# Gate and value as seven block products over parts of 512 tokens, with four of twelve column blocks beside the attention

## The chip, the core and the metric

The kernel runs on one core of a Trainium2 chip, in one launch. The metric is the device time of that launch in microseconds (us). The core has five instruction streams that run side by side and wait for each other through semaphores: PE (TensorE, matrix products into PSUM), DVE (VectorE), ACT (ScalarE), POOL (GpSimd) and SP (SyncE, which here only issues DMA transfers). PE, DVE and ACT can read or write PSUM as the program uses it here; POOL works on SBUF alone.

## The reference

Attention with feature maps in place of a softmax, then a gated layer on its output (cut to what is computed):

```python
def phi(x):
    proj = np.einsum('bhsd,df->bhsf', x, w_phi)
    proj = proj - np.max(np.abs(proj), axis=-1, keepdims=True)
    return np.concatenate([np.exp(proj), np.exp(-proj)], axis=-1)
q_p, k_p = phi(q), phi(k)                    # batch 8, heads 8, 576 tokens, 64 -> 2 x 128
kv = np.einsum('bhsf,bhsd->bhfd', k_p, v)
num = np.einsum('bhsf,bhfd->bhsd', q_p, kv)
den = np.einsum('bhsf,bhf->bhs', q_p, np.sum(k_p, axis=2))[..., None] + 1e-06
x = (num / den)                              # as (4608 tokens, 512)
xn = x / np.sqrt(np.mean(x * x, -1, keepdims=True) + 1e-06) * rms_g
g, val = xn @ w_gate, xn @ w_val             # 512 x 1536 each
out = (g / (1 + np.exp(-g)) * val) @ w_out   # 1536 x 512
```

The three large weights arrive as float64: the kernel reads them as pairs of 32-bit words and decodes them to float32 itself. The other inputs are float32.

## The kernel before, in words

Every matrix product in reduced float32 is made of three matmuls: each operand is split into a high part (a cast on ACT) and a low part (a subtraction on DVE or POOL; `_split`, L59), and high x high, high x low and low x high are summed in PSUM. There are three stages.

**Attention** (first 500 us). 32 pairs of heads pass a pipeline: `front` (transposes and projections), `mid` (exponentials, the sum over tokens), `back` (numerator and denominator), `last` (division, store of x to `xs` in DRAM). Between them run the pieces that decode weights, one per pair (`decode_pieces`), and *fill* units: for a block of 288 tokens whose x is in DRAM, `fill` (L460) splits x, and a unit (L467) computes one of the first `J1` = 3 column blocks of 128 columns, for gate or value, without the norm, in 12 matmuls 288 wide (L474), copies the sum out of PSUM (L477) and stores it to `gvs`. 16 blocks x 3 x 2 = 96 units. The rest of them run after the last pair (L533).

**Gate/value** (about 610 to 1067 us). 12 parts of `T` = 384 tokens. `prep` (L145) squares x, sums the squares by a matmul with ones, takes root and reciprocal (L159, L160), scales x (L162) and splits it. `gv` (L576) goes through the other nine column blocks: 12 matmuls 384 wide for the gate into one PSUM bank, 12 for the value into another (L588); then `hidden` (L569): SiLU on ACT, a product on DVE (L573), a store to `hs`. `gv_raw` (L593) fetches a block that the fill units computed, multiplies it by the reciprocal norm on DVE (L596) and finishes it in the same way; three per part. Pieces that decode w_out run beside this, and `load_o` prepares weights of the output stage.

**Output** (about 1067 us to the end). 18 groups of 256 tokens, each a 2 x 2 block product made of seven products instead of eight (`omm`, L737: 18 matmuls 256 wide each), with sums and differences of blocks formed on DVE and splits by ACT, DVE and POOL (L672 to L684).

The order of instructions on each engine is not that of the source: the framework simulates the program when it is built and places what it finds ready first. `late` ties some pieces behind the last instruction of an engine. A tile pool with `bufs=n` keeps n buffers of a name; a new one waits until the oldest is read. Each engine works off its own order strictly.

Of the kernel before, what the change touches and what calls it, by code (L numbers as in the profile page):

```python
# [82 lines left out]
def kernel(ctx: ExitStack, tc: tile.TileContext, q, k, v, w_phi,  # L83
# [13 lines left out]
    J1 = 3  # L97
    T = 384
    NB = N // T
    TF = S // 2  # L100
# [19 lines left out]
    x_ctx = ExitStack()  # L120
    wfp = x_ctx.enter_context(tc.tile_pool(name="wfp", bufs=1))
    wf1 = [[wfp.tile([128, NC, J1 * 128], F32R, name=f"f{n}{i}") for i in range(2)] for n in "gv"]
    xm = x_ctx.enter_context(tc.tile_pool(name="xm", bufs=1))
    xops = [x_ctx.enter_context(tc.tile_pool(name="xo0", bufs=1))]
    xips = [x_ctx.enter_context(tc.tile_pool(name="xip", bufs=1))]
# [13 lines left out]

    def fetch(bk, n=T):  # L140
        x = xips[-1 if bk % 2 else 0].tile([128, NC * T], F32, name="x")[:, 0:NC * n].rearrange("p (c t) -> p c t", c=NC)
        nc.sync.dma_start(out=x, in_=xsv[:, :, bk * n:(bk + 1) * n])
        return x

    def prep(bk, x, pool, name):  # L145
        ss = xm.tile([128, T], F32, name="ss", bufs=1)
        nc.scalar.activation(ss, x[:, 0], AF.Square)
        for c in range(1, NC):
            sq = xm.tile([128, T], F32, name="sq", bufs=1)
            nc.scalar.activation(sq, x[:, c], AF.Square)  # L150
            nc.gpsimd.tensor_tensor(ss, ss, sq, ALU.add)  # L151
        sp = pool.tile([128, T], F32, name=name)
        sh = xm.tile([128, T], F32R, name="sq", bufs=1)
        sl = xm.tile([128, T], F32R, name="fo", bufs=3)
        _split(nc, sh, sl, ss, lo_eng=nc.gpsimd)
        nc.tensor.matmul(sp[:, 0:T], ones, sh, start=True, stop=False)
        nc.tensor.matmul(sp[:, 0:T], ones, sl, start=False, stop=True)
        ri = xm.tile([128, T], F32, name="ri", bufs=2)
        nc.scalar.activation(ri, sp[:, 0:T], AF.Sqrt, scale=1.0 / DM, bias=eps)  # L159
        nc.vector.reciprocal(ri, ri)  # L160
        for c in range(NC):
            nc.vector.scalar_tensor_tensor(x[:, c], x[:, c], g[:, c:c + 1], ri, ALU.mult, ALU.mult)  # L162
        xhl = xops[bk % len(xops)].tile([128, 2, NC, T], F32R, name="xb")
        _split(nc, xhl[:, 0], xhl[:, 1], x, lo_eng=nc.gpsimd)
        return xhl[:, 0], xhl[:, 1], ri
# [334 lines left out]
    for i in range(PR + 3):  # L500
# [26 lines left out]
        if i == PR - 5:  # L527
            x0 = fetch(0)
# [272 lines left out]
```

## Time and profile before

| what | value |
|---|---|
| median of 3 runs | 1345.85 us (1344.51 to 1346.44) |
| span of the profiled execution | 1345.4 us |
| granted TensorE clock, mean | 0.991 |
| HBM read, written | 126.04 MB, 69.50 MB |
| longest waits of PE, in total | 9.8 us, 9 times (fill units, for a split of x on DVE); 7.6 us, once (output stage, for a cast on ACT); 4.6 us, once (gate/value, for a weight's cast on ACT) |

The page of the profile gives for the profiled execution its span, from the first to the last instruction, and no other time. A row of a group has the source line, the engine, the operation, output and inputs by the program's names, shapes, the count, then busy time in us, the mean duration of one in ns, and the engine's idle time just before them with what ended it. A row of a timeline has the start and the duration in us. A row of stretches has for each engine the busy time in us and the number of instructions, then the granted clock, the DMA share and GB/s. A row of the chain of waits has a start, a duration, an engine, a tile and a line.

### The profile page before, as it was taken

What the parts mean: (1) busy time and instruction counts of PE and PEld (TensorE: products, weight loads), DVE (VectorE), ACT (ScalarE), POOL (GpSimd) and SP (SyncE); (2) the same over time, 40 slices, a digit from 0 to 9 for tenths busy, and PEclk for the clock granted to TensorE, in tenths of its full rate; (3) what the DMA queues carried; (4) which work ended last, traced back from release to release, by engine and by line L of the source; (5) the groups of instructions that cost most, each with busy time, mean ns of one, the idle gap of its engine ahead of it and who ended that gap; (6) DMA issues with size and microseconds to landing.
All of it is one profiled execution on the core that took longest, in us unless ns stands there. A gap on an engine that the chain in (4) does not pass through costs nothing.

```text
span 1345.4 us, 25468 instructions
## 1 busy us (share of the span) xinstructions
PE 1291.3 (96%) x9396; PEld 1275.3 (95%) x9396; DVE 914.7 (68%) x1301; ACT 710.0 (53%) x1510; POOL 619.6 (46%) x568
## 2 busy tenths in 40 slices
PE   7989999999999997998999999999999799999998
PEld 7889899999999887998999999999999799999998
DVE  7899888778778762114566656655343489999995
ACT  5988877778778772334434434443332234344332
POOL 3766565555556660000223222222221078878885
PEclk9999999999999898999999999999999999999999
DMA  5455656565556434437454454454333434454351
GB/s 162 125 144 158 162 159 166 168 170 167 161 151 162 125 113 144 150 128 203 145 171 145 157 176 154 133 169 151 110 123 100 158 116 136 132 172 137 126 176 60
DMA packets 204523, 197.21 MB, mean 147 GB/s; under 512 B 69553, under 2 KB 186417, under 8 KB 204401
## 3 DMA queue, kind: packets, MB, share of 16 engines
q1 hardware_dynamic: 194896, 190.88, 47.0%
q10 hardware_dynamic: 9504, 4.72, 1.2%
q8 instruction: 74, 1.21, 0.4%
q14 instruction: 49, 0.39, 0.1%
HBM read 126.04 MB, written 69.50 MB: 145 GB/s over the span
## 4 chain that ended last, share of the span: by engine, by line
PE 80%; DVE 7%; DMA 5%; ACT 4%; issue 2%; POOL 2%; SPq 0%; ACTq 0%; DVEq 0%; POOLq 0%
PE fp L588 15%; PE gp L588 15%; PE fp L474 10%; PE acc L351 6%; PE gd L737 5%; PE gz L737 5%; PE gy L737 5%; PE sm L415 3%; PE fp L737 2%; PE pp L311 2%; PE fp L415 2%; PE pp L313 2%; PE pp L312 2%; PE sm L298 2%; PE sm L364 2%
## 5 line engine op out<-in xcount | busy, mean ns | idle before, releaser
L380 POOL TENSOR_TENSOR ql<-eq,qh 128x256 fp32r<-128x256 f32 x256 | 217.1, 879 | 67.2 <-issue 38.2
L61 POOL TENSOR_TENSOR xo<-st,xo 128x768 fp32r<-128x768 f32 x54 | 125.0, 2328 | 94.0 <-ACT xo L60 92.2
L588 PE MATMUL fp<-xb,wg 128*128 128x384 f32 x864 | 163.0, 336 | 4.6 <-ACT wg L60 4.6
L588 PE MATMUL gp<-xb,wv 128*128 128x384 f32 x864 | 161.5, 334 | 0.0
L588 PEld LDWEIGHTS fp<-xb,wg 128*128 128x128 f32 x864 | 151.9, 189 | 5.1 <-ACT wg L60 4.9
L573 DVE TENSOR_TENSOR h<-sl,gp 128x384 f32<-128x384 f32 x108 | 59.5, 551 | 135.0 <-PE gp L588 71.2
L588 PEld LDWEIGHTS gp<-xb,wv 128*128 128x128 f32 x864 | 150.8, 188 | 0.0
L571 ACT ACTIVATE sl<-fp 128x384 f32<-128x384 f32 x108 | 52.7, 489 | 167.4 <-PE fp L588 148.6
L54 POOL TENSOR_TENSOR wa<-raw,wa 128x192 f32<-128x192 f32 (+1 forms) x112 | 67.4, 622 | 159.5 <-issue 56.7
L351 PE MATMUL acc<-vm,ek 128*128 128x65 f32 x1024 | 131.6, 271 | 0.0
L315 DVE TENSOR_REDUCE mx<-pp 128x4 f32<-128x512 f32 (+1 forms) x160 | 100.5, 631 | 42.4 <-PE pp L313 41.1
L351 PEld LDWEIGHTS acc<-vm,ek 128*128 128x128 f32 x1024 | 127.8, 194 | 0.3 <-ACT ek L338 0.2
L60 ACT CAST xo<-st 128x768 fp32r<-128x768 f32 x54 | 43.4, 835 | 153.1 <-DVE st L675 76.9
L61 POOL TENSOR_TENSOR xb<-x,xb 128x1536 fp32r<-128x1536 f32 x12 | 42.7, 3562 | 152.0 <-ACT xb L60 152.0
L151 POOL TENSOR_TENSOR ss<-ss,sq 128x384 f32<-128x384 f32 x36 | 37.5, 1041 | 154.4 <-ACT sq L150 154.4
L474 PE MATMUL fp<-xo,fg 128*128 128x288 f32 x576 | 95.9, 303 | 9.8 <-DVE xo L61 9.8
L376 ACT ACTIVATE qh<-sm 128x512 fp32r<-128x512 f32 (+1 forms) x192 | 97.1, 506 | 0.0
L474 PEld LDWEIGHTS fp<-xo,fg 128*128 128x128 f32 x576 | 81.8, 190 | 13.2 <-DVE xo L61 12.2
L474 PE MATMUL fp<-xo,fv 128*128 128x288 f32 x576 | 92.5, 299 | 0.0
L61 POOL TENSOR_TENSOR xo<-ht,xo 128x768 fp32r<-128x768 f32 x36 | 91.6, 2545 | 0.0
L311 PE MATMUL pp<-wh,th 128*128 128x256 f32 x288 | 88.6, 309 | 2.7 <-DVE yr L318 2.1
L375 ACT ACTIVATE eq<-sm 128x512 f32<-128x512 f32 x128 | 78.2, 611 | 13.1 <-PE sm L364 12.0
(163 smaller groups left out, 3589.1 us busy)
## 6 DMA issues: line engine op xcount, KB each, us to landing
hs<-h SPq DMA_DIRECT2D x144, 192.0 KB
ht<-hs SPq DMA_DIRECT2D x18, 1536.0 KB
gvs<-fo SPq DMA_DIRECT2D x96, 144.0 KB
gvr<-gvs SPq DMA_DIRECT2D x36, 384.0 KB
rc<-di SPq DMA_DIRECT2D x32, 288.0 KB
x<-xs SPq DMA_DIRECT2D x16, 576.0 KB
x<-xs SPq DMA_DIRECT2D x12, 768.0 KB
kt<-in_k_dram SPq DMA_DIRECT2D x32, 256.0 KB
```

Of the source, the lines that this page charges most:

```text
L54: nc.gpsimd.tensor_tensor(a[:, h], lf[:, h], a[:, h], ALU.mult)
L61: (lo_eng or nc.vector).tensor_tensor(lo, x, hi.bitcast(F32), ALU.subtract)
L311: nc.tensor.matmul(o, th[:, cs], wh, start=True, stop=False)
L315: nc.vector.tensor_reduce(mx[:, 0:2 * m], pp[:, 0:2 * m], axis=AX.X, op=ALU.max, apply_absolute_value=True)
L351: nc.tensor.matmul(acc[:, sg, h], e[h][:, sg, j], vm[:, h, j], start=False, stop=(h == 1 and j == T0 - 1))
L375: nc.scalar.activation(ei[:, sg], yi, AF.Exp, scale=1.0 - 2.0 * sg)
L376: nc.scalar.activation(hi[:, sg], yi, AF.Exp, scale=1.0 - 2.0 * sg)
L380: nc.gpsimd.tensor_tensor(lo[:, sg, cs], ei[:, sg, cs], hi[:, sg, cs].bitcast(F32), ALU.subtract)
L415: nc.tensor.matmul(o[:, 0:SH], a[:, h, sg], e[:, sg, h, cs], start=(i == 0), stop=(i == 5))
L474: nc.tensor.matmul(fp[:, 0:TF], w, xx[x][:, c], start=(i == 0), stop=(i == 3 * NC - 1))
L588: nc.tensor.matmul(gp[:, 0:T], w, e[:, c], start=(i == 0), stop=(i == 3 * NC - 1))
L737: nc.tensor.matmul(place[n], a[:, kp], w[:, o], start=(first and kp == 0 and i == 0), stop=(kp == KP - 1 and i == 2), skip_group_check=True)
```

## The change

The gate and value products take the form that the output stage has already. A part is now 512 tokens, and there are 9 parts. The two halves of the model dimension and the two halves of the part's tokens make a 2 x 2 block matrix of x; gate and value of one column block make the other side. Seven products of six matmuls each, 256 wide, replace eight. Sums are built up in PSUM where they can be (the bank `pa` takes products 1, 6 and 7 one on the other, with a copy by ACT after each; `pe` takes 5 and 3), and four additions per column block on DVE form the results in SBUF.

- `J1` is 4: the fill units compute four of the twelve column blocks (128 units), `gv` the other eight. `RES`, the units held back during the attention, is 40.
- `blocks7` builds the seven weight blocks of a column block from one staging pair `w`, `t` (one buffer each): four sums on DVE, two casts on ACT, a split on DVE and one on POOL. Four such weights lie in `wA`, four in `wB`, which takes the place of the fill weights.
- `prep` is cut into ten pieces that run between column blocks; the blocks' sums are formed on DVE, and the splits' low parts alternate between POOL and DVE.
- The two products of `gv_raw` move from DVE to POOL; it runs four times per part.
- The six weights of the output stage are all prepared in the last part.
- After the attention, units run three at a time, with two pieces of the first part's preparation between them.

The core of the diff (the weight names, the pools and the attention's own lines are cut):

```diff
-    J1 = 3
-    T = 384
+    J1 = 4
+    T = 512
+    HT = T // 2
...
-        for c0 in range(n, DF, 384):
+        for c0 in range(n, DF, 512):
...
+    def blocks7(pool, load, names):
+        w = wst.tile([128, 4, CH], F32, name="w")
+        t = wst.tile([128, 4, CH], F32, name="t")
+        load(w)
+        sub = lambda o, a, b, op=ALU.subtract: nc.vector.tensor_tensor(t[:, o], a, b, op)
+        names(w, t, sub)
+        wt = pool.tile([128, 2, 7, CH], F32R, name="W")
+        _split(nc, wt[:, 0, 0:3], wt[:, 1, 0:3], w[:, 0:3])
+        _split(nc, wt[:, 0, 3:7], wt[:, 1, 3:7], t, lo_eng=nc.gpsimd)
...
-            for c in range(NC):
-                a, al = pl[0][:, c], pl[1][:, c]
-                for w, e in ((a, xh), (a, xl), (al, xh)):
-                    nc.tensor.matmul(gp[:, 0:T], w, e[:, c], start=(i == 0), stop=(i == 3 * NC - 1))
...
+        def mm(o, n, first):
+            xh, xl = x[n]
+            for c in range(2):
+                cs = slice(c * 128, (c + 1) * 128)
+                wh, wl = (w[:, i, ROW[n], cs] for i in range(2))
+                for i, (a, e) in enumerate(((wh, xh), (wh, xl), (wl, xh))):
+                    nc.tensor.matmul(o, a, e[:, c], start=(first and c == 0 and i == 0),
+                                     stop=(c == 1 and i == 2), skip_group_check=True)
...
+        mm(A, 1, True)
+        s1 = copy(A)
+        mm(Bk, 2, True)
+        nc.vector.tensor_tensor(G[:, 0:HT], Bk, s1, ALU.add)
+        while pend:
+            pend.pop()()
+        mm(A, 6, False)
+        u2 = copy(A)
+        mm(E, 5, True)
+        mm(Dk, 4, True)
+        mm(A, 7, False)
+        u3 = copy(A)
+        nc.vector.tensor_tensor(V[:, HT:T], E, u3, ALU.add)
+        nc.vector.tensor_tensor(V[:, 0:HT], u3, Dk, ALU.subtract)
+        def third():
+            mm(E, 3, False)
+            nc.vector.tensor_tensor(G[:, HT:T], E, u2, ALU.add)
+            hidden(sb, J1 + j, G, V, V, nc.vector)
+        pend.append(third)
...
-        nc.vector.tensor_tensor(r, r, xb[bk][2].unsqueeze(1).broadcast_to([128, 2, T]), ALU.mult)
-        hidden(bk, j, r[:, 0], r[:, 1])
+        nc.gpsimd.tensor_tensor(r, r, xb[sb]["ri"].unsqueeze(1).broadcast_to([128, 2, T]), ALU.mult)
+        hidden(sb, j, r[:, 0], r[:, 1], r[:, 1], nc.gpsimd)
```

How the built programs differ shows best in the middle of the gate/value stage. On DVE, around the reciprocal of the norm, the program before has these rows (`h` is gate x value, `gvr` a block from the fill units, `wp` and `wa` the decoding of w_out):

```order
L55 TENSOR_TENSOR wa<-wp,wa 128x256
L573 TENSOR_TENSOR h<-sl,gp 128x384
L573 TENSOR_TENSOR h<-sl,gvr 128x384
L160 RECIPROCAL ri<-ri 128x384
L162 SCALAR_TENSOR_TENSOR x<-x,g,ri 128x384 x4
L596 TENSOR_TENSOR gvr<-gvr,ri 128x768
L573 TENSOR_TENSOR h<-sl,gp 128x384 x2
L50 TENSOR_SCALAR wp<-wa 128x256
```

The changed program has these on DVE at the same point of a later part (`G` and `V` are gate and value, `pb`, `pe` and `pd` are PSUM banks, `u` is a copy of the bank `pa`):

```order
L655 TENSOR_TENSOR G<-pb,u 128x256
L594 RECIPROCAL ri<-ri 128x512
L671 TENSOR_TENSOR G<-pe,u 128x256
L597 SCALAR_TENSOR_TENSOR x<-x,g,ri 128x512 x3
L666 TENSOR_TENSOR V<-pe,u 128x256
L667 TENSOR_TENSOR V<-u,pd 128x256
L597 SCALAR_TENSOR_TENSOR x<-x,g,ri 128x512
L50 TENSOR_SCALAR wp<-wa 128x256
L627 TENSOR_TENSOR V<-G,V 128x512
```

Readings of PSUM banks (L655, L671, L666, L667) now stand between and behind the reciprocal and the scalings; before, DVE read one bank per column block there, and nothing else of PE's.

On POOL, one part of the stage before has these rows (`ss` and `sq` are squares, `xb` is the split of x, `wa` the decoding):

```order
L151 TENSOR_TENSOR ss_10528<-ss_10528,sq_10533 128x384
L151 TENSOR_TENSOR ss_10528<-ss_10528,sq_10536 128x384
L61 TENSOR_TENSOR fo_10541<-ss_10528,sq_10540 128x384
L54 TENSOR_TENSOR wa_10363<-raw_10246,wa_10363 128x128 x2
L54 TENSOR_TENSOR wa_10479<-raw_10360,wa_10479 128x128 x2
L61 TENSOR_TENSOR xb_10553<-x_10412,xb_10553 128x1536
L54 TENSOR_TENSOR wa_10621<-raw_10476,wa_10621 128x128 x2
```

The changed program has these on POOL, about half of one part (`gvr` is a block from the fill units, `xo` a split of a block of x):

```order
L678 TENSOR_TENSOR gvr_13780<-gvr_13780,ri_13398 128x1024
L61 TENSOR_TENSOR xo_13552<-x_13176,xo_13551 128x512
L627 TENSOR_TENSOR gvr_13780<-gvr_13780 128x512
L54 TENSOR_TENSOR wa_13408<-raw_13239,wa_13408 128x128 x2
L678 TENSOR_TENSOR gvr_13910<-gvr_13910,ri_13398 128x1024
L61 TENSOR_TENSOR xo_13589<-t2_13486,xo_13588 128x512
L627 TENSOR_TENSOR gvr_13910<-gvr_13910 128x512
L61 TENSOR_TENSOR xo_13624<-x_13176,xo_13623 128x512
```

The multiplications of the finished blocks (L678, L627) are new on POOL and stand between the splits that PE's next part needs.

On PE, one column block of the changed program in the middle of the stage reads so (each row is one product of six matmuls, or two for x12; `pa` is one of two banks, as is `pe`):

```order
L639 MATMUL pd<-xo,W 128x256 x6
L639 MATMUL pb<-xo,W 128x256 x6
L639 MATMUL pa<-xo,W 128x256 x6
L639 MATMUL pe<-xo,W 128x256 x6
L639 MATMUL pa<-xo,W 128x256 x12
```

These are product 4 of a block, 2 of the next, 7 of the first, 5 of the next, and then 1 of the block after that and 6 of the next; the first block's product 3, which adds to the bank `pe` that DVE must have read after product 7, comes right behind them. Before, a block was 12 matmuls into one bank and 12 into another, with nothing to wait for in between.

More of the change, by code (lines that the diff above doesn't have):

```diff
@@ L533, with gv_raw @@
+    def gv_raw(sb, j):
+        r = wk.tile([128, 2, T], F32, name="gvr", bufs=1)
+        nc.sync.dma_start(out=r, in_=gvv[j][:, :, sb * T:(sb + 1) * T])
+        nc.gpsimd.tensor_tensor(r, r, xb[sb]["ri"].unsqueeze(1).broadcast_to([128, 2, T]), ALU.mult)
+        hidden(sb, j, r[:, 0], r[:, 1], r[:, 1], nc.gpsimd)
+    xb = {0: {}}
+    first, then = prep(0, fetch(0), xb[0])
+    ahead = [lambda: load_gv(0)] + first + then + [lambda j=j: load_gv(j) for j in (1, 2, 3)]
     while units or here or fills:
@@ L535 @@
             landed()
-        now, units[:] = units[:6], units[6:]
+        now, units[:] = units[:3], units[3:]
+        now.append(lambda: [ahead.pop(0)() for _ in range(2) if ahead])
         _merge([now])
         load_x()
-    a_ctx.close()
-    g_ctx = ExitStack()
-    rg = ctx.enter_context(tc.tile_pool(name="rg", bufs=1, reuse_waits="tile", side="right"))
-    dec = g_ctx.enter_context(tc.tile_pool(name="m_dec", bufs=1, reuse_waits="tile"))
-    xips.pop()
-    xops += [g_ctx.enter_context(tc.tile_pool(name=f"xo{i}", bufs=1, reuse_waits="tile")) for i in (1, 2)]
@@ L626 @@
[L626 to L643 removed]
+    while ahead:
+        ahead.pop(0)()
@@ new lines, with after @@
+    f_ctx.close()
+    wp[1] = ctx.enter_context(tc.tile_pool(name="wB", bufs=4, reuse_waits="tile", side="right"))
+    dec = g_ctx.enter_context(tc.tile_pool(name="g_dec", bufs=1, reuse_waits="tile", side="right"))
+    decs = decode_pieces(decs_late, dec)
+    wos_ops = []
+    for sb in range(NB):
+        lasts = []
+        def after(n):
+            if n != 3 and lasts:
+                lasts.pop(0)()
+        for j in range(JN):
+            if sb == 0 and j + 4 < JN:
+                load_gv(j + 4)
+            gv(sb, j, after if j == JN - 1 else lambda n: None)
+            if j % 2 == 1:
+                gv_raw(sb, j // 2)
+            if j == 1 and sb + 1 < NB:
+                xb[sb + 1] = {}
+                first, lasts = prep(sb + 1, fetch(sb + 1), xb[sb + 1])
+            elif 3 <= j < 6 and sb + 1 < NB:
+                first.pop(0)()
+            elif j == 6 and sb + 1 < NB:
+                lasts.pop(0)()
+            if sb and j % 2 == 0 and decs:
+                decs.pop(0)()
+            if sb == NB - 1 and 0 < j and len(wos_ops) < KP:
+                wos_ops.append(load_o(len(wos_ops)))
+        while lasts:
+            lasts.pop(0)()
```

251 lines of the change are left out of this document (127 added, 124 removed).

## The prediction

> **What bounds the kernel now.** I read the page's busy times first, then stretches of the span, then the chain of waits.
>
> ```profile
> span 1345.4 us, 25468 instructions
> PE 1291.3 (96%) x9396; PEld 1275.3 (95%) x9396; DVE 914.7 (68%) x1301; ACT 710.0 (53%) x1510; POOL 619.6 (46%) x568
> ```
>
> ```profile
> core 0: us, PE busy (x) PEld busy (x) DVE busy (x) ACT busy (x) POOL busy (x), PEclk, DMA share, GB/s
> 400.00:450.00 50.00, 46.58 (x386) 45.43 (x384) 44.23 (x77) 41.78 (x104) 29.46 (x34) 1.00 0.63 171
> 450.00:500.00 50.00, 49.70 (x377) 49.20 (x376) 35.23 (x51) 40.64 (x95) 36.91 (x43) 0.93 0.29 87
> 500.00:550.00 50.00, 39.17 (x272) 37.78 (x273) 10.76 (x17) 13.41 (x30) 0.00 (x0) 0.93 0.50 156
> 660.00:1060.00 400.00, 400.00 (x2309) 400.00 (x2309) 217.94 (x334) 151.64 (x270) 98.31 (x96) 1.00 0.44 143
> 1110.00:1330.00 220.00, 220.00 (x1904) 219.82 (x1903) 206.93 (x154) 86.41 (x124) 188.84 (x79) 1.00 0.43 140
> ```
>
> In the gate/value stage (660 to 1060) PE never rests, DVE works 54% of the time and POOL 25%. In the output stage, which already uses seven products, PE never rests either, but DVE shows 94% and POOL 86%. The chain is PE almost throughout:
>
> ```profile
> 363.09 3.17 PE fp L474 x24
> ...
> 596.23 9.83 PE fp L474 x71
> ...
> 670.37 2.08 PE gp L588 x12
> 672.80 2.08 PE fp L588 x12
> ...
> 1064.88 2.10 PE gp L588 x12
> 1067.03 6.56 DMA ht<-hs
> ...
> 1165.85 2.08 PE fp L737 x18
> ```
>
> So 12 matmuls 384 wide take 2.08 us, 18 that are 256 wide also 2.08 (a product of six: 0.693), and a fill matmul 288 wide 3.17/24 = 0.132. Gaps of 0.35 (672.80 less 670.37 less 2.08) are the two matmuls of the norm.
>
> The sum is made against this execution's span, 1345.4, which is 0.45 below the median of the runs shown; the page gives no other time of it.
>
> **The change part by part.** (1) PE's gate/value work. Before: 12 parts x (9 blocks x 2 x 2.08 + 0.35) = 453.5. After: 9 parts x (8 blocks x 7 x 0.693 + 0.46 for the norm's matmuls, 512/384 of 0.35) = 353.6. **-99.9.**
>
> (2) The fourth column block beside the attention: 16 blocks x 2 units x 12 matmuls x 0.132 = **+50.7**, since PE is the limit wherever fill runs.
>
> (3) The last pairs had few units; the order now gives them about three each. PE's idle time from 400 to 550 is 3.4 + 0.3 + 10.8 = 14.5. Bounds 0 and -14.5; I take **-9**, as part of it is the latency of the last pair.
>
> (4) Decode pieces of 512 columns, 24 instead of 32.
>
> ```profile
> 153.70:167.90 14.20, 13.26 (x107) 12.47 (x106) 11.60 (x22) 11.26 (x29) 8.52 (x11) 1.00 0.66 178
> ```
>
> A pair without fill takes 14.2 with DVE 11.6 busy. A third more decoding is some 0.7 us of DVE work on 16 such pairs: between 0 and +11. **+4**, nearer to nothing, as DVE has 2.6 idle.
>
> (5) The start of the stage. Its 453.5 ended at 1066.98, while the last fill ended at 606.06: 7.4 were lost to weight loads. Now four of eight blocks run among the fill units, but the other four weights lie where the fill weights lay, and pass one staging buffer, one by one. Copying and splitting one after another I put at 12 lost, between 2 (all hidden) and 20: **+5**.
>
> (6) DVE beside POOL, which decides. Prices first.
>
> ```profile
> L573 DVE TENSOR_TENSOR h<-sl,gp 128x384 f32<-128x384 f32 x96 | 52.9, 551 | 127.7 <-PE gp L588 71.2 <-DMA hs<-h 42.4 <-ACT sl L571 6.4
> L160 DVE RECIPROCAL ri<-ri 128x384 f32<-128x384 f32 x10 | 25.5, 2547 | 0.0
> L50 DVE TENSOR_SCALAR wp<-wa 128x256 int32<-128x256 int32 x23 | 20.9, 908 | 0.0
> L61 DVE TENSOR_TENSOR wl<-wc,wh 128x768 fp32r<-128x768 f32 x5 | 4.8, 952 | 0.0
> ...
> L756 DVE TENSOR_TENSOR ro<-gz,uu 128x256 f32<-128x256 f32 x16 | 6.8, 424 | 0.6
> ```
>
> ```profile
> 861.90 0.55 DVE L573 TENSOR_TENSOR h<-sl,gp 128x384 f32<-128x384 f32 x1
> 862.37 0.55 DVE L573 TENSOR_TENSOR h<-sl,gvr 128x384 f32<-128x384 f32 x1
> 862.83 2.54 DVE L160 RECIPROCAL ri<-ri 128x384 f32<-128x384 f32 x1
> 865.41 2.21 DVE L162 SCALAR_TENSOR_TENSOR x<-x,g,ri 128x384 f32<-128x384 f32 x4
> ...
> 870.14 0.56 DVE L573 TENSOR_TENSOR h<-sl,gp 128x384 f32<-128x384 f32 x1 [1.16 <-ACT wa L48]
> 870.62 2.28 DVE L50 TENSOR_SCALAR wp<-wa 128x256 int32<-128x256 int32 x1
> ...
> 895.58 0.29 DVE L50 TENSOR_SCALAR wp<-wa 128x256 int32<-128x256 int32 x1
> 895.90 0.42 DVE L51 SCALAR_TENSOR_TENSOR wp<-wa,wp 128x256 int32<-128x256 int32 x1
> ```
>
> ```profile
> 869.22 3.53 POOL L61 TENSOR_TENSOR xb<-x,xb 128x1536 fp32r<-128x1536 f32 x1 [7.69 <-ACT xb L60]
> ```
>
> Operations in a row start 0.08 sooner than they last (861.90, 862.37). An estimate from these rows, per part of 512 tokens: 32 additions out of PSUM at 0.34 (L756 less 0.08) = 10.9; eight products of gate and value, 512 wide, at 0.61 (between the rows for 384 and 768) = 4.9; reciprocal 2.55 x 4/3 = 3.4; four scalings at 0.69 (2.21/4 x 512/384, less the fixed share) = 2.75; seven sums and splits at 0.61 = 4.3; in parts 1 to 6 four decodes of 1.35 = 5.4. That is 31.7 against PE's 39.3, so averages say that it fits. Two things speak against it.
>
> First, the work is uneven. The order shows reciprocal, scalings, sums, splits and two decodes in four of the eight blocks: 20.7 us of DVE there against PE's 19.9. It cannot be lent to the other blocks: PE needs DVE's read of a block's bank pe before the third product, three products (2.08) after the block's last copy.
>
> Second, POOL. L50 took 0.29 when POOL rested (895.58), and 2.28 at 870.62: it ended at 872.90, just after POOL's operation of 869.22 to 872.75. The h of 870.14, with an operand in PSUM, was not held. In the output stage the same holds all the time:
>
> ```profile
> L61 DVE TENSOR_TENSOR xo<-ht,xo 128x768 fp32r<-128x768 f32 x30 | 50.4, 1718 | 0.0
> L673 DVE TENSOR_TENSOR ht<-ht 128x768 f32<-128x768 f32 x15 | 37.3, 2490 | 0.5
> L680 DVE TENSOR_TENSOR st<-ht,st 128x768 f32<-128x768 f32 x16 | 33.2, 2072 | 3.5 <-POOL xo L61 3.5
> L672 DVE TENSOR_TENSOR st<-ht 128x768 f32<-128x768 f32 x15 | 32.5, 2167 | 8.4 <-DMA ht<-hs 6.7 <-POOL xo L61 1.7
> L675 DVE TENSOR_TENSOR st<-ht 128x768 f32<-128x768 f32 x15 | 22.4, 1496 | 0.0
> ```
>
> Against 0.95 alone (the 768 of L61 above) six such operations average 1.94: each is held up 1.0 by a POOL that is 86% busy. POOL's price:
>
> ```profile
> L61 POOL TENSOR_TENSOR xb<-x,xb 128x1536 fp32r<-128x1536 f32 x10 | 35.8, 3577 | 111.7 <-ACT xb L60 111.7
> L151 POOL TENSOR_TENSOR ss<-ss,sq 128x384 f32<-128x384 f32 x28 | 29.0, 1037 | 50.2 <-ACT sq L150 50.2
> L54 POOL TENSOR_TENSOR wa<-raw,wa 128x128 f32<-128x128 f32 x48 | 22.0, 479 | 97.6 <-issue 52.0 <-ACT sl L571 31.3 <-DVE wa L52 14.3
> ```
>
> That is 2.2 ns per element and 0.19. The four finished blocks, moved to POOL, are 4 x (2.4 + 1.3) = 14.8; squares and splits 8 x 1.3 = 10.4; decodes 8 x 0.45 = 3.6: 28.8 per part, against 98/400 of the time now. POOL is busy 60% of a part of 49, and 35 of DVE's operations have all operands in SBUF. The hold-up of one lies between 0 (they miss each other) and 1.0 (the output stage); I take 0.4, which is 0.6 times half to two thirds of POOL's usual 1.3. The heavy blocks hold 22 of the 35: 20.7 + 22 x 0.4 = 29.5 against 19.9, so PE waits 9.6 per part. The light blocks (11 + 13 x 0.4 = 16.2 against 19.4) wait for nothing. Parts 1 to 6: 57.6; part 7, which decodes nothing, 6; part 0, whose preparation overlaps the waits of (5), 8. **+71.6**; with the bounds 0 and 1.0, +5 to +170.
>
> The trace shows POOL and DVE taking turns at such operations; if they did so without any loss, their times would add up: DVE's 35 (4.9 + 2.75 + 4.3 + 5.4 = 17.3) and POOL's 28.8 make 46.1 per part, 6.8 over PE, in parts 1 to 6, and less than PE's 39.3 in part 7. That is +41 in place of +71.6, and a rival below. The Trainium skill speaks against the change in the same place: "SBUF — State Buffer", section "Who interferes with whom", says that a DVE operation with two SBUF inputs and a GpSimd operation that reads SBUF exclude each other for the whole instruction, and that whichever issues first has the ports. By that rule, the trace agrees: the L50 of 870.62 ended with POOL's operation.
>
> ```profile
> L742 ACT COPY os<-fp 128x256 f32<-128x256 f32 x16 | 5.8, 360 | 0.0
> ```
>
> (7) ACT: copies out of PSUM now stand in PE's way. The tightest is the third of a block, one product (0.69) before PE needs its bank back; this copy of the same size lasts 0.36. Twice per part a load of a function table, and seven splits, stand among such copies in ACT's queue. Between 0 and +40 (the third rival): **+5**.
>
> (8) The end: in part 8 there is nothing to prepare, but all six weights of the output stage pass the one staging buffer, each with four differences and a split on DVE (4 x 0.34 + 0.87 = 2.2) and a split on POOL. They stand ahead of the ht load on SP's queue, which in the chain was the next thing after PE's last product, at 1067.03. Between -4 (all done before PE is) and +15 (two of them after it): **+4**. The rest of the output stage is unchanged.
>
> Sum: -99.9 + 50.7 - 9 + 4 + 5 + 71.6 + 5 + 4 = +31.4, so 1345.4 + 31.4 = **1377**.
>
> **The rivals.**
> *DVE keeps up (faster).* All terms but (6) make -40.2. If a hold-up is some 0.1, as in the stage now (POOL busy a quarter), each heavy stretch costs 20.7 + 2.2 - 19.9 = 3.0, with parts 0 and 7 some 21 in all: 1345.4 - 40.2 + 21 = **1326**; at no hold-up 1310. For it: only 0.8 is missing without contention, and POOL's operations wait for DVE's results, so that they may take turns. Against: 870.62 and the output stage. It decides at a hold-up of 0.21, where (6) is 40.
>
> *POOL holds ACT, ACT holds PE (slower still).* A finished block's SiLU waits on ACT for POOL's multiplication, with PE's copies behind it. If each of the 36 costs PE 1.1 more, with SP's queue held by the one gvr buffer: 1377 + 40 = **1417**. Against: the order places them well ahead of their need.
>
> *Turns without loss (no change).* With +41 for (6): 1345.4 - 40.2 + 41 = **1346**. For it: 870.62, where one waits exactly as long as the other runs. Against: DVE's order is fixed, so that it stands still at the head of its queue, with readings of PSUM behind it that POOL would not hold.
>
> ```profile
> L737 PEld LDWEIGHTS gy<-wh,xo 128*128 128x128 f32 x432 | 66.9, 188 | 0.4 <-ACT xo L60 0.2
> ```
>
> That the products do not run at 0.693, because weight loads show, would be 3024 x (0.188 - 0.116) us = +218 by the 188 ns of a load in this row; the output stage, with the same shapes, runs 18 in 2.08, so this gets no chance of its own.
>
> **How the numbers follow.** DVE bound at a hold-up of 0.25 to 0.7 (stalls of 6.3 to 16.2 per part, 1352 to 1426): 0.48. DVE keeps up: 0.32. POOL through ACT: 0.10. Turns without loss: 0.10, half of it within 2.7 us of 1345.4 and a quarter on either side. The first is the forecast, 1377. The range must reach into the second, so 1312 to 1425; the likeliest case's own is 1352 to 1426. Within 0.2% (2.7 us), about what a measurement of this kernel can tell from no change, lies only that half: faster 0.32 + 0.03 = 0.35, same 0.05, slower 0.48 + 0.10 + 0.02 = 0.60.
>
> **What would show it.** Right: in the gate/value stage PE's idle time is put down to DVE's readings of pe and pd, at once per part, in a stretch beginning with the reciprocal; the 512-wide DVE operations last well over 0.69; parts take about 49 and parts 7 and 8 less. Products inside a block still start 0.116 per matmul apart. The forecast is wrong if PE is busy through as it is now, if part lengths do not follow the preparation, or if the waits name ACT or a DMA.

## The result and the profile after

| | before | changed |
|---|---|---|
| median of four runs | 1345.87 us | 1458.24 us |
| range | 1344.51 to 1346.44 | 1448.25 to 1460.38 |
| ratio | 1 | 1.0807, 95% interval 1.0765 to 1.0848 |
| span of the profiled execution | 1345.4 us | 1458.3 us |

Slower, as forecast, but by 112 us where 31 were forecast; the time lies 33 us beyond the range. The page after, its first lines and one group:

```profile
span 1458.3 us, 27581 instructions
...
PE 1309.4 (90%) x10206; PEld 1275.9 (87%) x10206; DVE 1079.7 (74%) x1513; ACT 798.9 (55%) x1730; POOL 816.1 (56%) x650
...
L627 DVE TENSOR_TENSOR V<-G,V 128x512 f32<-128x512 f32 x72 | 76.1, 1058 | 35.6 <-ACT G L626 35.6
```

No engine is full now. Stretches of the changed kernel (length, busy time of each engine, granted clock): the first products among the last fill units, the rest of part 0, the parts after it, the last part, and a piece of the output stage; then the same places before:

```profile
500.00:697.00 197.00, 170.70 (x1218) 166.75 (x1217) 75.75 (x92) 81.09 (x175) 54.82 (x38) 0.94 0.43 138
697.00:767.00 70.00, 49.24 (x310) 45.46 (x309) 45.97 (x64) 31.33 (x58) 38.05 (x22) 0.83 0.38 120
767.00:1092.30 325.30, 273.17 (x2030) 259.47 (x2028) 264.94 (x408) 162.82 (x351) 190.47 (x140) 0.94 0.44 142
1092.30:1175.00 82.70, 68.17 (x537) 64.66 (x536) 63.33 (x104) 40.04 (x79) 39.84 (x20) 1.00 0.37 121
1210.00:1410.00 200.00, 200.00 (x1699) 199.99 (x1699) 190.87 (x139) 79.49 (x111) 172.77 (x72) 1.00 0.45 146
```

```profile
500.00:606.00 106.00, 94.25 (x666) 90.66 (x666) 17.90 (x27) 34.29 (x78) 3.80 (x4) 0.97 0.44 144
606.00:1067.00 461.00, 455.65 (x2615) 454.11 (x2614) 250.91 (x384) 180.24 (x318) 104.45 (x100) 1.00 0.46 147
1110.00:1310.00 200.00, 200.00 (x1731) 199.82 (x1730) 188.80 (x140) 78.95 (x113) 170.66 (x72) 1.00 0.45 145
```

Between 500 us and the last gate/value product, take off the matmuls at their median distances in the trace. Before: 567 less 666 x 0.133 and 2615 x 0.173 leaves 26 us. Changed: 675 less 3042 x 0.119 (products and norms) and 1053 x 0.133 (fill) leaves 173. The products did get cheaper as said; what PE loses beside them grew by 147, where the terms (3), (5), (6) and (7) of the prediction make it 73 (-9 + 5 + 71.6 + 5). What PE waited for, from the first product on (total, times, longest):

```profile
PE pa L639 <- ACT u L645: 30.0, 40, 2.5
PE pe L639 <- DVE V L666: 29.3, 17, 4.5
PE pe L639 <- DVE G L671: 8.8, 8, 1.3
PE pa L639 <- DVE W L61: 7.5, 4, 2.5
PE fp L445 <- ACT fo L448: 7.1, 5, 2.6
PE pa L639 <- ACT W L60: 6.3, 4, 2.8
PE pb L639 <- DVE G L655: 5.3, 6, 2.0
```

DVE's readings of PSUM (L666, L671, L655) are named for 43.4 us in all, ACT's copies `u` for 30.0, as much as L666 alone. One stall of a part, on DVE and on POOL (start, duration):

```profile
937.93 3.35 DVE L594 RECIPROCAL ri<-ri 128x512 f32<-128x512 f32 x1 [1.18 <-ACT ri L593]
941.20 0.36 DVE L671 TENSOR_TENSOR G<-pe,u 128x256 f32<-128x256 f32 x1
941.48 4.20 DVE L597 SCALAR_TENSOR_TENSOR x<-x,g,ri 128x512 f32<-128x512 f32 x3
945.60 0.41 DVE L666 TENSOR_TENSOR V<-pe,u 128x256 f32<-128x256 f32 x1
```

```profile
941.42 2.38 POOL L678 TENSOR_TENSOR gvr<-gvr,ri 128x1024 f32<-128x1024 f32 x1 [5.94 <-DVE ri L594]
```

POOL's multiplication starts 0.06 ahead of the scalings; three of them take 4.20 where, with POOL at rest, four take 2.73 in the last kernel of experiment 5. PE's next product waits behind them for L666. What follows on PE, and then stretches around it (length, PE's busy time and count, granted clock, DMA share, GB/s):

```profile
942.43 0.87 PE L639 MATMUL pa<-xo,W 128*128 128x256 f32 x6
946.07 1.25 PE L639 MATMUL pe<-xo,W 128*128 128x256 f32 x6 [2.77 <-DVE V L666]
947.12 1.48 PE L639 MATMUL pd<-xo,W 128*128 128x256 f32 x6
948.40 1.48 PE L639 MATMUL pa<-xo,W 128*128 128x256 f32 x6
```

```profile
943.00:946.00 3.00, 0.29 (x3) 1.00 0.00 0
946.00:947.00 1.00, 0.93 (x6) 0.78 0.00 0
947.00:950.00 3.00, 2.88 (x14) 0.50 0.00 0
950.00:953.00 3.00, 2.66 (x22) 1.00 0.45 175
```

After a stall of 2.77 the clock falls to half for 3.4 us: products start 1.28 apart, not 0.71. By the starts of all matmuls between the first norm and the last product, those 0.18 to 0.26 apart cost 38.5 us over 0.116 each. In the kernel before, the granted clock is 1.00 from 614 us to the last product. No term of the sum had this.

Not every stall of this length is followed by a slow stretch. In the last part PE comes back from a longer one at full clock:

```profile
1108.76 0.98 PE L639 MATMUL pe<-xo,W 128*128 128x256 f32 x6 [2.83 <-DVE V L666]
```

In the trace of the changed kernel the stretches at half clock begin at whole multiples of 3.413 us from each other. On that grid, the starts of the matmuls give an estimate of how far each window is filled (0.119 us for a matmul, 0.133 in a fill unit, or less if the next one starts sooner). From the first norm to the last product, 18 windows at full clock were followed by half clock, all filled to at most 0.41; the 139 others at full clock were filled to at least 0.41. The stall that ended at 946.07 lay in one window, filled to 0.12; the one that ended at 1108.76 lay across two, filled to 0.61 and 0.45.

### The profile page after: what moved, and what is told of

Same layout as the page of the kernel before. It is cut to its first block, busy times and chain, and to the rows that moved or that the text cites. A ratio compares the mean times of both kernels' runs of the same rounds, so it can differ in the third digit from the quotient of the medians.

```text
span 1458.3 us, 27581 instructions
## 1 busy us (share of the span) xinstructions
PE 1309.4 (90%) x10206; PEld 1275.9 (87%) x10206; DVE 1079.7 (74%) x1513; ACT 798.9 (55%) x1730; POOL 816.1 (56%) x650
## 4 chain that ended last, share of the span: by engine, by line
PE 31%; DVE 9%; issue 6%; DMA 6%; POOL 3%; ACT 2%; ACTq 0%; SPq 0%; POOLq 0%; DVEq 0%
PE gd L814 5%; PE gz L814 5%; PE gy L814 5%; PE fp L445 5%; PE pa L639 4%; DMA x<-xs 3%; PE pe L639 3%; PE fp L814 2%; DVE x L597 2%; DMA gvr<-gvs 1%; PE pd L639 1%; PE pb L639 1%; DVE V L627 1%; DVE xo L61 1%; POOL gvr L678 1%
## 5 line engine op out<-in xcount | busy, mean ns | idle before, releaser
L639 PE MATMUL pa<-xo,W 128*128 128x256 f32 x1296 | 202.2, 298 | 46.6 <-ACT u L645 30.0
L639 PEld LDWEIGHTS pa<-xo,W 128*128 128x128 f32 x1296 | 178.8, 202 | 59.1 <-ACT u L645 39.6
L639 PE MATMUL pe<-xo,W 128*128 128x256 f32 x864 | 138.1, 297 | 41.1 <-DVE V L666 29.3
L639 PEld LDWEIGHTS pe<-xo,W 128*128 128x128 f32 x864 | 120.3, 201 | 47.7 <-DVE V L666 33.0
L678 POOL TENSOR_TENSOR gvr<-gvr,ri 128x1024 f32<-128x1024 f32 x36 | 90.5, 2514 | 110.5 <-DMA gvr<-gvs 47.2
L645 ACT COPY u<-pa 128x256 f32<-128x256 f32 x216 | 74.1, 370 | 112.7 <-PE pa L639 109.9
L54 POOL TENSOR_TENSOR wa<-raw,wa 128x256 f32<-128x256 f32 (+1 forms) x96 | 78.2, 834 | 74.4 <-DVE wa L52 50.9
L445 PEld LDWEIGHTS fp<-xo,fv 128*128 128x128 f32 x768 | 109.6, 192 | 4.3 <-ACT fo L448 3.9
L627 DVE TENSOR_TENSOR V<-G,V 128x512 f32<-128x512 f32 x72 | 76.1, 1058 | 35.6 <-ACT G L626 35.6
L448 ACT COPY fo<-fp 128x288 f32<-128x288 f32 x128 | 51.2, 405 | 81.3 <-PE fp L445 62.9
```

Of the source, the lines that this page charges most:

```text
L54: nc.gpsimd.tensor_tensor(a[:, h], lf[:, h], a[:, h], ALU.mult)
L445: nc.tensor.matmul(fp[:, 0:TF], w, xx[x][:, c], start=(i == 0), stop=(i == 3 * NC - 1))
L627: eng.tensor_tensor(out_, a, v, ALU.mult)
L639: nc.tensor.matmul(o, a, e[:, c], start=(first and c == 0 and i == 0), stop=(c == 1 and i == 2), skip_group_check=True)
L678: nc.gpsimd.tensor_tensor(r, r, xb[sb]["ri"].unsqueeze(1).broadcast_to([128, 2, T]), ALU.mult)
```

## Experiments

All times are medians of four runs (five for one, named there). "Four parts" is a stretch between two norms with 1355 matmuls, 161 us of them at 0.119; in the changed kernel:

```profile
825.90:1043.50 217.60, 182.83 (x1355) 173.62 (x1353) 178.06 (x271) 109.65 (x236) 130.15 (x95) 0.94 0.44 144
```

**1. The fourth block's units left out.** (Code here and below is shortened. In this run `RES` and the units per pair follow the smaller number, and the finished block 3 is read from block 2's values.)

```diff
-        return [lambda j=j, wi=wi: unit(j, wi) for j in range(J1) for wi in range(2)]
+        return [lambda j=j, wi=wi: unit(j, wi) for j in range(UJ) for wi in range(2)]   # UJ = 3
```

> The changed kernel with only three of its four column blocks worked beside the attention; the finished block 3 of the gate/value stage is read from block 2's values, so that everything else is done as often as before (the fourth block's own values are left out). Theory A (PE is the limit wherever fill runs, as the prediction said): 384 matmuls less at 0.132 us make it some 45 to 55 us shorter, about 1408 against 1458. Rival B (in the drain the waits of the first gate/value blocks set the time, and the fill units only fill them): 15 to 35 us shorter, 1423 to 1443. Either way the gate/value stage behind the last fill stays within 5 us of its 478.

1409.56 us, 48.7 less: theory A. The last gate/value product ends 483.6 behind the last fill, 477.8 in the changed kernel, just beyond the 5 us of change that were expected. So terms (2) and (3), +41.7 together, were 48.7. Most of the -9 for idle time of the last pairs did not come, as far as this one run can tell the two terms apart.

**2. POOL's multiplications left out, or replaced by writes.** (The first piece of code is against the changed kernel, the second against the first.)

```diff
-        nc.gpsimd.tensor_tensor(r, r, ...ri..., ALU.mult)
-        hidden(sb, j, r[:, 0], r[:, 1], r[:, 1], nc.gpsimd)
+        nc.scalar.activation(r[:, 0], r[:, 0], AF.Silu)
+        nc.sync.dma_start(out=hsv[...], in_=r[:, 0])
```

> The changed kernel without POOL's two multiplications of the finished blocks (gvr times ri, and times the value): only SiLU of the raw gate values is stored, so the first four blocks of hs are left out. POOL loses 36 x (2.5 + 1.5) = some 144 us. Theory A (POOL holds DVE's SBUF operations, and they hold PE): steady parts fall from 54.7 to 51 or less, the whole to 1425 or less; DVE's scalings come back to some 0.7 us each. Rival B (DVE's own work in the reciprocal's stretch and ACT's queue set the stalls): parts stay above 53, the whole above 1445.

1414.25 us, theory A; four parts:

```profile
821.30:1008.80 187.50, 171.53 (x1355) 164.85 (x1354) 151.31 (x273) 102.67 (x223) 62.74 (x64) 0.99 0.31 109
```

```diff
+        for _ in range(2):
+            nc.gpsimd.memset(r, 0.5)
         nc.scalar.activation(r[:, 0], r[:, 0], AF.Silu)
+        for _ in range(3):
+            nc.gpsimd.memset(r[:, 1], 0.5)
-        nc.sync.dma_start(out=hsv[...], in_=r[:, 0])
+        nc.sync.dma_start(out=hsv[...], in_=r[:, 1])
```

> The changed kernel with POOL's two multiplications of the finished blocks replaced by fills with a constant of about the same length on POOL (gvr twice, its value half three times: some 4.0 us per block, as before), behind the same transfer and the same SiLU; hs of the first four blocks is left out. POOL stays as busy and its queue as long, but these spans read no SBUF. Theory A (what holds DVE is that both read SBUF): as without them, steady parts about 46, the whole 1410 to 1428. Rival B (POOL's queue is the limit: the low parts of the splits and the transfer of x come late behind the finished blocks): parts 53 or more, the whole above 1445.

1392.89 us, 65 less, 17 below even theory A. The four parts take as long as without POOL's work (188.6, 187.5); the 21 us between the two runs lie mostly ahead of these four parts, and what makes them wasn't followed up. Four parts, with POOL as busy as in the changed kernel (61% of the stretch, 60% there); then groups on DVE in both kernels over their four parts:

```profile
801.80:990.40 188.60, 173.92 (x1355) 166.30 (x1353) 145.44 (x273) 106.90 (x236) 114.17 (x145) 0.98 0.51 168
```

```profile
L50 DVE TENSOR_SCALAR wp<-wa 128x256 int32<-128x256 int32 x16 | 12.8, 801 | 0.0
L597 DVE SCALAR_TENSOR_TENSOR x<-x,g,ri 128x512 f32<-128x512 f32 x16 | 11.4, 768 | 0.0
```

```profile
L627 DVE TENSOR_TENSOR V<-G,V 128x512 f32<-128x512 f32 x31 | 27.1, 873 | 6.1 <-ACT G L626 6.1
L597 DVE SCALAR_TENSOR_TENSOR x<-x,g,ri 128x512 f32<-128x512 f32 x16 | 22.0, 1412 | 0.0
L50 DVE TENSOR_SCALAR wp<-wa 128x256 int32<-128x256 int32 x16 | 20.0, 1253 | 0.0
L51 DVE SCALAR_TENSOR_TENSOR wp<-wa,wp 128x256 int32<-128x256 int32 x16 | 14.7, 918 | 0.0
...
L55 DVE TENSOR_TENSOR wa<-wp,wa 128x256 f32<-128x256 f32 x15 | 11.6, 774 | 5.9 <-POOL wa L54 5.4
L52 DVE TENSOR_SCALAR wa<-wp 128x256 int32<-128x256 int32 x16 | 11.5, 720 | 0.0
L61 DVE TENSOR_TENSOR xo<-t,xo 128x512 fp32r<-128x512 f32 x4 | 5.8, 1449 | 0.0
```

The last fence is the changed kernel. Against 0.68, 0.69, 0.29, 0.42, 0.43, 0.28 and 0.68 undisturbed, these seven groups were held up 6.0 + 11.6 + 15.4 + 8.0 + 5.2 + 7.0 + 3.1 = 56 us in four parts; the other operations of this kind were not. That is 0.40 for each of 35 a part, the value that the prediction took. The timelines show it operation by operation. In the changed kernel, 60 of the 91 that ran beside a span of POOL lasted over 0.15 longer than undisturbed, and none of the 48 that met no such span. With the writes in place, 23 of 34 beside one of POOL's other operations, which read SBUF, were held, and 2 of 46 beside writes alone, both L50; the hold-ups of four parts fall from 56 to 21 us. The Trainium skill, "SBUF — State Buffer", section "Who interferes with whom", draws the line there too: two SBUF inputs on DVE contend with an operation of GpSimd that reads SBUF, not with one that only writes it. The trace agrees for L597. L50, with one SBUF input, was held as well, by 0.96 on average; the section allows it for forms that run in a two-port mode, and no run here shows in which mode it ran. The L50 of 870.62, which the prediction set beside the rule for two inputs, is therefore no case of that rule; the scalings of L597 are.

**3. The multiplications on DVE.**

```diff
-        nc.gpsimd.tensor_tensor(r, r, ...ri..., ALU.mult)
-        hidden(sb, j, r[:, 0], r[:, 1], r[:, 1], nc.gpsimd)
+        nc.vector.tensor_tensor(r, r, ...ri..., ALU.mult)
+        hidden(sb, j, r[:, 0], r[:, 1], r[:, 1], nc.vector)
```

> The changed kernel with the two multiplications of the finished blocks on DVE, where the kernel before has them; nothing is left out. DVE gains 4 x (1.2 + 0.7) = 7.6 us of its own per part, POOL loses 16. Theory A (a hold-up costs DVE more than the work itself): parts fall to about 50, the whole to 1415 to 1435. Rival B (DVE is full in the reciprocal's stretch whoever holds it): parts stay at 54 or grow, the whole 1455 or more.

1412.67 us, 45.6 less: theory A, 2 us beyond its range; four parts:

```profile
801.60:998.70 197.10, 176.49 (x1355) 167.02 (x1353) 172.24 (x302) 107.43 (x234) 63.53 (x65) 0.98 0.48 161
```

With 8 us a part more to do DVE is busy for less time than in the changed kernel (172.2 for 178.1): the work costs it less than the hold-ups did, which fall from 56 to 21 us in four parts here too.

**4. Waits of ACT, and no preparation at all.**

```diff
-                first, lasts = prep(sb + 1, fetch(sb + 1), xb[sb + 1])
+                first, lasts = prep(sb + 1, x0, xb[sb + 1])
```

> The changed kernel without the fetch of x for parts 1 to 8: each preparation works on what stands in x already (the values of those parts are wrong), with the same operations. ACT's squares no longer stand waiting for the transfer of 8.0 us ahead of the copies that PE needs. Theory A (the wait for x costs 2.5 us of stall per part, and as much again in products at half rate behind it): steady parts fall from 54.7 to about 49.5, the whole by 30 to 40 us, to about 1423. Rival B (the preparation's other steps take up the time, and PE then waits for DVE instead): parts above 53, the whole above 1445.

1452.23 us: theory B for the whole, though a part takes 52.2 (208.7 us for four), not over 53. Without the wait for x, which the trace names behind stalls of 2.5, the median is 6 us shorter, with ranges that overlap; ACT's copies are still named for 35.9 us of PE's waits over 700 to 1100, 26.9 in the changed kernel.

```diff
-                first, lasts = prep(sb + 1, fetch(sb + 1), xb[sb + 1])
+                xb[sb + 1] = xb[sb]        # and none of its pieces is called
```

> The changed kernel with the preparation of parts 1 to 8 left out (all parts use part 0's operands, so that their values are wrong): no squares, reciprocal, scalings, sums or splits beside the products; the finished blocks, the decodes and all copies and additions stay. Theory A (PE's stalls come of the preparation, held up by POOL): parts fall to 40 to 43, the whole to 1345 to 1375. Rival B (the short reserve of PSUM banks and the finished blocks stall PE even without it): parts 45 or more, the whole above 1385.

1423.96 us, theory B. A stall of that kernel, on POOL, ACT and PE:

```profile
909.75 2.40 POOL L678 TENSOR_TENSOR gvr<-gvr,ri 128x1024 f32<-128x1024 f32 x1 [7.58 <-DMA gvr<-gvs]
```

```profile
912.19 0.63 ACT L626 ACTIVATE gvr<-gvr 128x512 f32<-128x512 f32 x1 [3.57 <-POOL gvr L678]
912.72 0.61 ACT L626 ACTIVATE G<-G 128x512 f32<-128x512 f32 x1
913.24 0.35 ACT L645 COPY u<-pa 128x256 f32<-128x256 f32 x1
```

```profile
913.65 0.98 PE L639 MATMUL pa<-xo,W 128*128 128x256 f32 x6 [1.34 <-ACT u L645]
```

The finished block's SiLU stands at the head of ACT's queue for POOL, and PE's copy behind it: the prediction's third rival, at work beside its forecast. POOL in turn waits for a transfer into the one buffer `gvr`. In the changed kernel itself ACT waits for this operation of POOL 19 times, 33.5 us in all and 4.5 at most.

**5. Taking that round apart.**

```diff
-        r = wk.tile([128, 2, T], F32, name="gvr", bufs=1)
+        r = wk.tile([128, 2, T], F32, name="gvr", bufs=2)
```

> The changed kernel with two buffers gvr in place of one; nothing is left out. Without the preparation the parts still took 49 us, PE waiting for ACT's copies, ACT for POOL's multiplication of gvr, and that for a transfer into the one buffer that the last store had just freed: some 12.4 us a round, against 10.1 of PE for two blocks. Theory A (this round sets the pace of the parts): steady parts fall from 54.7 to 47 to 50, the whole to 1400 to 1425. Rival B (the reading of SBUF by POOL and DVE sets it, and the buffer only moves the wait): parts above 52, the whole 1440 or more.

1454.68 us, theory B. PE's waits over 760 to 1030 of that kernel:

```profile
PE pe L639 <- DVE V L666: 25.4, 9, 4.8
PE pa L639 <- ACT u L645: 15.8, 15, 3.0
```

With the buffer alone the longest waits are for DVE. Why is not shown: the hold-ups of DVE are about as before, 59 us in four parts against 56.

With the second buffer and the multiplications on DVE (both edits):

> Two buffers gvr, and the finished blocks' multiplications on DVE; nothing is left out. Theory A (the two causes add up, the round and the hold-up): steady parts 44 to 47, the whole 1378 to 1400. Rival B (with the multiplications on DVE the round is short enough already): as on DVE alone, 1405 to 1418.

1427.33 us: neither; 15 longer than on DVE alone. The scheduler puts the instructions in another order, with 18 us of waits for L671; why the shift is for the worse was not followed up.

```diff
-            if j % 2 == 1:
-                gv_raw(sb, j // 2)          # fetch, multiplications and SiLU
+            if j % 2 == 0:
+                gv_raw(sb, j // 2)          # the fetch alone
+            elif raws:
+                gv_done(*raws.pop(0))       # the rest, on DVE, within late()
```

> As the run with two buffers and DVE, but each finished block is fetched one block sooner and its multiplications and SiLU are issued behind the next block's copies and additions, so that ACT never stands waiting for them; nothing is left out. Theory A (what is left of PE's waits is ACT standing at the head of its queue for finished blocks): 8 to 20 us shorter than that run. Rival B (the waits that are left come of the reciprocal's stretch and of part 0): within 5 us of it.

1386.26 us, 41 less than the run before it, more than theory A's 20. With its twin in experiment 8 it is the shortest here that leaves nothing out (1.0295 of the kernel before, 1.0271 to 1.0318); no run that leaves nothing out beats the kernel before. Four parts, and PE's waits over 760 to 1030:

```profile
781.50:976.80 195.30, 173.92 (x1355) 163.11 (x1353) 178.76 (x305) 107.09 (x238) 62.15 (x65) 1.00 0.51 162
```

```profile
PE pa L639 <- ACT u L645: 12.0, 25, 0.5
PE pe L639 <- DVE V L666: 8.1, 15, 1.2
```

No wait is longer than 1.2 now, and the granted clock is 1.00. DVE's hold-ups, 22 us in four parts, are what they were in experiment 3, and the four parts are only 2 us shorter than there; of the 26 us between that run and this one, 20 lie between the first norm and the third. DVE is busy for 92% of the four parts.

**6. What is left.** As the run before, without preparation (edit as in 4):

> As the run with the finished blocks later (two buffers, DVE, 1386.3 us), with the preparation of parts 1 to 8 left out (their values are wrong). Theory A (what is left of the stalls comes of the preparation: the reciprocal, scalings and splits ahead of readings of PSUM): parts fall from 48.5 to 41 to 43, the whole to 1315 to 1340. Rival B (the order of the products and the copies by ACT between them stall PE anyway): parts 45 or more, the whole above 1350.

1338.78 us (five runs), 0.9934 of the kernel before (0.9906 to 0.9963): theory A, nearly at its upper end. 200 us of it hold 1593 matmuls, 42.2 for a part, which has 336 without its norm:

```profile
750.00:950.00 200.00, 191.69 (x1593) 187.94 (x1593) 141.20 (x307) 83.06 (x209) 16.91 (x38) 1.00 0.51 163
```

So with the finished blocks out of the way the preparation costs the remaining 47 us, and even a free one would gain less than 1% on the kernel before.

On top of that kernel of experiment 5, with its preparation, first the products held to the order of the code, then the reciprocal in two halves as well:

```diff
+            with in_turn():        # issue_after the last instruction of PE
+                mm_(o, n, first)
```

> As the run with the finished blocks later, with PE's products held to the order of the code (1, 2, the third of the block before, 6, 5, 4, 7), so that two products stand between any copy by ACT and the next use of its bank, and all fill units stand ahead of the first product; nothing is left out. Theory A (the scheduler's order, which puts products 6 and 7 side by side in places and first products among fill units, costs PE): 10 to 25 us shorter than 1386. Rival B (the products wait for DVE's readings whatever their order): within 5 us, or longer, as PE can no longer pass a product that waits.

```diff
-            nc.vector.reciprocal(ri, ri)
+            for h in range(2):
+                nc.vector.reciprocal(ri[:, h * HT:(h + 1) * HT], ri[:, h * HT:(h + 1) * HT])
```

> As the run with products in turn, with the reciprocal of 512 columns (3.35 us) in two halves of 256, between which DVE can read PSUM; nothing is left out. Theory A (the reciprocal is the longest stretch in which DVE reads nothing for PE): 4 to 12 us shorter than that run. Rival B (the scheduler puts the halves side by side, or the scalings are as long a stretch): within 4 us.

1405.61 us: theory B, 19 longer. Held to its order PE can't pass a product that waits: over 760 to 1030 it waits 32.9 us for DVE's reading into V, 8.1 above. With the halves 1412.42 us: 7 longer again, neither theory (B was within 4). Halving the reciprocal gives nothing there; those waits stay at 32.0.

**7. The start.** Units first, and the preparation of part 0 and its first weights behind them:

```diff
-        now, units[:] = units[:3], units[3:]
-        now.append(lambda: [ahead.pop(0)() for _ in range(2) if ahead])
+        now, units[:] = units[:6], units[6:]
```

> The changed kernel with the preparation of part 0 and its first four weights issued behind the fill units, not among them; nothing is left out. By the order no gate/value product then stands between fill units. Theory A (the waits of the interleaved products cost PE more than they save: 25 us of waits between 548.6 and 696.9): the last fill ends near 650, and the whole is 10 to 25 us shorter, 1433 to 1448. Rival B (those waits only move behind the last fill, as the operands and weights of part 0 are then late there): within 8 us of 1458.

1456.84 us: theory B. Fill and part 0 of that kernel:

```profile
548.60:652.50 103.90, 98.47 (x730) 97.36 (x730) 20.65 (x38) 38.80 (x83) 9.61 (x4) 1.00 0.46 148
652.50:755.00 102.50, 71.14 (x479) 66.74 (x478) 72.08 (x96) 47.97 (x91) 63.33 (x34) 0.80 0.37 118
```

The fill runs through, and what it gains is lost behind it.

```diff
-                load_gv(j + 4)
+                W[j + 4] = W[j]
```

> The changed kernel in which blocks 4 to 7 of the gate/value stage use the weights of blocks 0 to 3 again, so that four weights are not loaded, differenced and split in part 0 (those blocks' values are left out). Theory A (the single staging buffer's chain sets the second half of part 0): the 70.1 us between the second and third norm fall to 40 to 46, the whole by 20 to 32 us to 1426 to 1438. Rival B (part 1's preparation and the finished blocks set it): less than 10 us shorter.

> As the run with the finished blocks later (1386.3 us), with blocks 4 to 7 using the weights of blocks 0 to 3 again (their values are left out), so that four weights are not loaded, differenced and split in part 0. From the first norm to the third that run took 183.7 us for 153 of matmuls. Theory A (what is left of the start is the weights' chain through one staging buffer): 160 to 168 us there, the whole 15 to 22 us shorter. Rival B (it is the latency of part 0's own preparation and the fill units' waits): less than 8 us shorter there.

The edit alone and the edit on top of experiment 5's last kernel. The whole can't be read from these two (1465.95 and 1405.73 us, 8 and 19 longer): blocks 4 to 7 now hold the first weight buffers to the end, the output stage's weights come late (in the second run three of the six are fetched from 1101.30 on, behind the last gate/value product, which ends at 1094.0), and its first group takes 35 and 43 us instead of some 20. The stretch from the first norm to the third can be read. In the changed kernel its second half falls from 70.1 to 37.5 us, even below theory A, but the first half grows by 16, and the whole stretch falls from 218.4 to 201.4 only. In the other it falls from 183.7 to 181.8, theory B: there PE waits for part 1's operands instead, 7.62 at 704.99 and 1.60 at 707.39. (The 6.31 of the second row stands before part 0's first products, where experiment 5's last kernel has it too.)

```profile
PE pa L639 <- ACT xo L60: 8.2, 2, 7.6
PE pa L639 <- POOL xo L61: 7.9, 2, 6.3
```

**8. Matmuls 0.119 apart.** In the output stage, whose code is unchanged, 126 matmuls take 14.84 us, 14.56 before, at a granted clock of 1.00 both times (1699 and 1731 in 200 us above). First the weights in two tiles, as before, then ht and xo at other addresses:

```diff
-        wt = pool.tile([128, 2, 7, CH], F32R, name="W")
+        wh = pool.tile([128, 7, CH], F32R, name="Wh")
+        wl = pool.tile([128, 7, CH], F32R, name="Wl")
```

> The changed kernel with the high and low parts of each seven-block weight in two tiles of 7 KB, as the output stage's weights are in the kernel before, in place of one of 14 KB; nothing is left out. In the output stage 18 matmuls take 2.12 us where they took 2.08, at the same places in each product. Theory A (it is the place of the operands in SBUF): the groups go back to about 2.08, the whole gets 4 to 14 us shorter. Rival B (it is not the layout of the weights): 2.12 stays, the whole within 5 us of 1458.

```diff
+    ow = ctx.enter_context(tc.tile_pool(name="ow", bufs=2, reuse_waits="tile"))
     ohp = ctx.enter_context(tc.tile_pool(name="ohp", bufs=2, reuse_waits="tile"))
     xop = ctx.enter_context(tc.tile_pool(name="oop", bufs=16, reuse_waits="tile"))
-    ow = ctx.enter_context(tc.tile_pool(name="ow", bufs=2, reuse_waits="tile"))
```

> As the run with the finished blocks later (1386.3 us), with the output stage's pools opened in the order of the kernel before (ow ahead of ohp and oop), so that ht and xo lie at other addresses; nothing is left out. Theory A (the addresses of the operands set the 113 to 121 ns of a matmul): the groups of 18 change from 2.12 us, to 2.08 if the old places were good ones, and the whole gets some 5 us shorter. Rival B (they have no part in it): 2.12 stays, the whole within 3 us of 1386.

1455.49 us, and 1384.73 us on top of experiment 5's last kernel, groups of 14.84 in both: theory B twice. The cause stays open.

## Why the prediction missed

The direction was right and for the reason that was given; the size was not. The step that failed is the lost time of PE: 73 us in the sum, 147 measured. It had no term for PE's half speed behind a stall (38.5 us), put the start at 20 where PE lost 65, and gave ACT's queue 5.

- **(1) Products, -99.9:** right but for 0.119 in place of 0.116 a matmul, which is 3024 x 0.003 = 9 us.
- **(2) The fourth block, (3) idle time used:** 48.7 by experiment 1, +41.7 forecast.
- **(4) Decoding, +4:** mis-sized where it was read, and gone at the end. The first 12 pairs of heads have no fill units in either kernel; the 13th pair's first `acc` matmul starts at 190.2 us, 179.0 before. Those 11 us are the upper bound that the prediction gave. The decoding then ends at 372 us, 490 before, and at 500 us the matmuls left differ by 387, the 384 of the fourth block and 3 more: by then the loss has been made up.
- **(5) The start:** the step that was furthest off. From first to third norm PE loses 218.4 - 720 x 0.133 - 480 x 0.119 = 65 us, where the working had 20 (12 for the weights, and 8 for part 0 in (6)). The weights were sized about right: PE's waits there name them for 15.0, and without four of them the stretch is 17 shorter. The working left out the rest: 15 us of half speed, 9.7 of waits of the fill units for their copies and splits, 7.5 for part 0's and part 1's operands, 10.3 for readings and copies of PSUM, and smaller gaps. In experiment 5's last kernel the stretch is 35 shorter. That is not POOL's multiplications alone: without them (experiment 2) it takes 222.7.
- **(6) DVE beside POOL, +71.6:** right in mechanism (experiments 2 and 3) and in the price of a hold-up, 0.40. Both of its factors hold: 91 of 139 operations met a span of POOL, 0.65 for the 0.6 taken, and one that did was held 0.62 on average, for 0.65 to 0.87. From the third norm on, waits and delays of over 0.26 us come to 82 us, where (6) without part 0 and (7) had 69. But the same stalls then run into the clock: 23 us more there, 15 in the start. **That PE comes back from a stall at half speed is the missing term**, 38.5 us of the 81; how much of it would otherwise have been waiting for DVE wasn't tried.
- **(7) ACT, +5:** wrong in size. Its copies are named for 30 us of PE's waits. The third rival was held off by "the order places them well ahead of their need"; an order shows places, not times, and ACT waited 33.5 us for POOL at these places.
- **(8) The end, +4:** from the last gate/value product to the first of the output stage 5.6 us, 7.5 before. So the wait that (8) sized did not grow. Behind it the first group takes 20.2, 17.4 before, and most other groups are 0.28 longer by the distance of the matmuls: 5.1 in all behind the last gate/value product.
- **What was to show it:** the waits on pe begin at the reciprocal and part lengths follow the preparation, as said. Steady parts took 54.4, not 49, and the waits name ACT, which the prediction had set down as a sign against it; two rivals held at once, and a sum for each alone was too small.

The whole miss is 81 us: the terms missed by 147 - 73 = 74 in lost time, some 10 in the price of matmuls and 1 behind the last product, and 4 the other way for (4).

## What to carry to other kernels

Work that is moved from a busy DVE to an idle POOL isn't free: where both read SBUF, DVE's operations were held up in these runs, and here 8 us a part back on DVE made the kernel 46 us faster, though still slower than the kernel before. What waits for another engine belongs behind the copies and readings that TensorE needs next, in the same queue. A stall of TensorE of over 2 us is to be priced with the slow products that may follow it, and averages of busy time (74%, 55%, 56%) tell of none of this.

## What the runs showed of the hardware

- Between the first norm and the last product of the changed kernel PE's granted clock fell to 0.50 eighteen times, mostly within 0.7 us of the end of a stall of 2 to 3 us, and stayed there for 3.4 us or a multiple of it. It fell after windows of 3.413 us that matmuls filled to at most 0.41, so a stall of 2.77 inside one window was enough and one of 2.83 across two was not. The Trainium skill, "TensorE: Matmul & The Clock Gate", section "Part 1: The HAM clock gate (the "warmup" mystery)", puts the fall after an idle window of about 3.4 us that runs freely. The trace agrees with the length of the window and that it runs freely; it does not agree that the whole window has to be idle. What the chip counts in a window, and so where its limit lies, no run here shows: 0.41 is an estimate from the starts of matmuls.
- The same 256-wide matmuls settle at 14.84 or 14.56 us for 126, each to the hundredth over a whole stage, by something that neither operand's address explained.
